# Loading the first key tile of a decode kernel as eight strided loads, with one of them at the head of the load queue

## The chip, the cores and the metric

The kernel runs on one core of a Trainium2 chip. The metric is the device time of one execution in microseconds (us), the median of several runs. Lower is better.

## What is computed

The reference is one decode step of two identical layers. Each layer is an attention block over a key and value cache, followed by a mixing block and an MLP. Batch is 2, there is one query position, the model width D is 576, and there are 32 heads of 128 columns over 16384 cached positions.

```python
def _A_ref(x, k_cache, v_cache, wq, wo):
    q = (x @ wq).reshape(B, Sq, H, Dh).transpose(0, 2, 1, 3)
    scores = jnp.einsum("bhqd,bhkd->bhqk", q, k_cache) * (Dh ** -0.5)
    p = _softmax(scores, axis=-1)
    o = jnp.einsum("bhqk,bhkd->bhqd", p, v_cache)
    return o.transpose(0, 2, 1, 3).reshape(B, Sq, H * Dh) @ wo
...
x = x + _A_ref(_layernorm(x), A_k_cache, A_v_cache, A_wq, A_wo)
x = x + _B_ref(_layernorm(x), B_w1, B_w2, B_w3, B_w4)
x = x + _A_ref(_layernorm(x), A_k_cache, A_v_cache, A_wq, A_wo)
x = x + _B_ref(_layernorm(x), B_w1, B_w2, B_w3, B_w4)
```

Both layers read the same two caches. Each cache is 268 MB, and each layer reads both of them nearly whole, which is almost all of the data that the kernel moves.

## The kernel before

**Tiles.** A unit of work is one pair of heads of one batch entry, so that a layer has 32 units. The keys of a unit are one tile of 128 partitions by 65,536 bytes, 8.4 MB: each of the two heads fills 64 partitions, and each partition takes 256 consecutive positions, which are 64 KB in a row in memory. The values have the same form. The text calls such tiles "a K" and "a V". On-chip memory has room for three of them, in slots that `plan_all` names V, A and C (numbers 0, 1 and 2).

**The order of loads.** All loads are issued by one queue, that of SyncE (SP), in the order in which `plan_all` (L549) lists them in a plan. `Store.pump` (L289) walks through the plan: an entry with a name must find its place free of other owners, and then becomes a load (`Graph.dma`, L85, issued in L98) that writes the memory cells of its place. An entry without a name (`None`) is issued without asking who owns its place, and writes the keys that it lists. The plan starts with the first 128 rows of the query weights wq, then the input x ("xin", two rows), the other four pieces of wq, and the mixer weights w2 in two loads, of which the second goes to the upper 64 partitions only. wq and w2 stand where the first V will be. After them come the tiles: K 0 into slot C, K 1 into slot A, V 0 into slot V as soon as wq and w2 have been used, then K 2 into slot A in two halves as K 1 is used up, and so on, K and V in turn.

**How dependencies become waits.** `Graph._add` (L49) records for each operation the last writer and the readers of each memory cell that it touches. A load that writes a cell which another load wrote depends on that load, though both are issued by the same queue. `Graph._waits` (L118) turns dependencies into semaphore waits, which the queue makes before it issues the load (L182). The semaphore of a load rises by 16 for each of its parts.

**The work.** In `landed` (L1321) GpSimd waits for a tile's load and passes the news on to TensorE and VectorE (the trace shows this as POOLq L187). Then `unit`, in `attention` (L1127), computes the scores of a K tile: a part of it on TensorE (transposes L1414, products L1452), the rest on VectorE (L1499 and L1509, in the first unit L1484 and L1488). The softmax follows, and in the next unit the values are weighted on TensorE (`pv`, L1569, products in L1578). `used` (L1377) and `release` (L329) free the cells that have been consumed, and `release` calls `pump` for the next loads. Before the first unit stand the layer norm of x, the query projection from wq (L930 and L940), a projection from w2 (L993) and the spreading of the first query vector (L1350, L1363, L1367).

The functions that the change touches and what calls them:

Of the kernel before, what the change touches and what calls it, by code (L numbers as in the profile page):

```python
# [338 lines left out]
class KB:  # L339
# [209 lines left out]
    def plan_all(self):  # L549

        B, D = self.B, self.D
        row, w3r, wqr = 2 * D, 2 * self.F, 2 * 128 * self.H
        g = [row * n + CELL for n in self.GROUPS[1]]
        self.cuts, self.korder = {}, {}
        s = [self.slot(i) for i in range(self.NSLOT)]
        source = {"k": self.K, "v": self.V}

        tiles = self.tile_order(0)
        V, A, C = range(3)
        assert tiles[:2] == [("k", 0), ("k", 1)]  # L560
        assert tiles[-3:] == [("k", self.W - 1), ("v", self.W - 2), ("v", self.W - 1)]
        full = lambda k, m, at: (k, 0, m, at)
        hd, mt = self.H, self.MT
        self.store.plan(None, "xin", 0, 0, [(self.rows[0:B, :], self.A_x.rearrange("b s d -> (b s) d"))], ["prod"])
        self.plan_cols("wq", 0, self.wq, [full(k, hd, s[V] + wqr * k) for k in range(self.KT)])
        first = self.store.queue
        first[0], first[1] = first[1], first[0]
        self.plan_small("w2", 0, self.w2, s[V] + wqr * (self.KT - 1) + wqr // 2, (0, 64))
        q = self.TILE // 4
        two = [(2 * q * j, 2 * q) for j in range(2)]  # L570
        assert tiles[3] == ("k", 2)
        for i, (t, u) in enumerate(tiles):
            last = i == len(tiles) - 1
            self.plan_tile(source[t], t, u, C if i == 0 or last else A if t == "k" else V, self.LAST_V if last else two if i == 3 else None)
        r8 = row * self.HG
        assert r8 == w3r

        def halves(n, pieces):
            return [(k, (h or 0) * n // 2, n if h != 0 else n // 2, at) for k, h, at in pieces]
        w = self.WINDOW  # L580
        self.plan_heads(0, w["wo"], 2)
        self.plan_cols("w3", 0, self.w3, halves(mt, w["w3"]))
        self.plan_groups(0, w["w4"])
        self.plan_cols("wq", 1, self.wq, halves(hd, w["wq"]))

        tiles = self.tile_order(1)
        assert tiles[:2] == [("k", self.W - 2), ("k", 0)] and tiles[2] == self.partly()
        tiles[:3] = tiles[2], tiles[0], tiles[1]
        e = self.HOLD * self.CH * 256
        self.plan_tile(source["k"], *tiles[1], A, [(0, e)])  # L590
        self.plan_tile(source["v"], *tiles[0], V, self.REST)
        self.plan_tile(source["k"], *tiles[1], A, [(e, q - e)] + [(q * j, q) for j in range(1, 4)])
        self.plan_tile(source["k"], *tiles[2], C, two)
        assert tiles[4][0] == "v" and tiles[5][0] == "k"
        for i, (t, u) in enumerate(tiles[3:]):
            self.plan_tile(source[t], t, u, C if i == len(tiles) - 4 else A if t == "k" else V, two if i in (1, 2) else None)
        assert t == "v"
        a = s[V]
        ats = []
        for _, lo, hi in self.cuts["wo", 0][-2:]:  # L600
            ats.append(row * (hi - lo))
        ats = [r8] * (self.ng - 1) + ats
        ats = [a + sum(ats[:i]) for i in range(len(ats))]
        self.plan_heads(1, ats)
        a += r8 * self.ng
        self.plan_small("w1", 1, self.w1, a, (0, 64))
        a += row * self.KT
        self.plan_cols("w3", 1, self.w3, [full(k, mt, a + w3r * k) for k in range(self.KT)])
        a += w3r * (self.KT - 1) + w3r // 2
        assert a % CELL == 0 and a + sum(g) <= self.size  # L610
        self.plan_groups(1, [a + sum(g[:i]) for i in range(len(g))], CELL)
# [1055 lines left out]
```

## Time and profile before

| what | value |
|---|---|
| median of 3 runs | 2544.99 us |
| lowest and highest run | 2544.64 and 2546.85 us |
| the profiled execution's own time | 2544.06 us |
| its span, from first to last instruction | 2542.3 us |
| mean granted TensorE clock | 0.639 of full speed |
| read from main memory | 1092.44 MB |

The profile is of one execution. Its views are these. The page has the busy time of each engine (PE is TensorE, PEld its weight loads, DVE VectorE, ACT ScalarE, POOL GpSimd, SP SyncE), the span in 40 equal slices with the busy share in tenths, and the DMA queues. The chain of waits follows the work that ended last back to what released it. The timeline lists instructions with their start and duration, where a q behind an engine's name means its instruction queue. The stages view gives busy time, granted clock, the busy share of the 16 DMA engines and the rate in GB/s for stretches of time. The DMA view counts packets by size in such a stretch and gives the time that they took as a share of 16 engines' time. A packet is counted with its whole time and size where it starts, so that in a short stretch the share can exceed 100%.

### The profile page before, as it was taken

To read this page: it belongs to the slowest core of one execution; us is meant where nothing else is said; L and a number is where in the kernel's file an instruction comes from. 1 tells how busy PE (TensorE), PEld (TensorE's weight loads), DVE (VectorE), ACT (ScalarE), POOL (GpSimd) and SP (SyncE) were. 2 spreads that over 40 slices of the span, in tenths; PEclk is the share of its full clock that TensorE was granted. 3 is DMA by queue.
4 is the path that set the end of the run, shared out by engine and by line. 5 is a ranking of instruction groups with operands and counts; after the bars stand their busy time and mean duration, and the time that the engine had idled before them with its cause. 6 is when DMAs were issued, how large, how long until landed. Compare 5 with 4: busy or idle time off the path is not lost.

```text
span 2542.3 us, 74308 instructions
## 1 busy us (share of the span) xinstructions
PE 1426.8 (56%) x34671; PEld 1335.1 (53%) x34671; DVE 1766.0 (69%) x1122; ACT 1125.9 (44%) x1705; POOL 29.6 (1%) x100
## 2 busy tenths in 40 slices
PE   4655654654655555556678555555465465555555
PEld 3554554544554545545567555455455455455555
DVE  4876866866767767768439777686686686776773
ACT  3553453543544534534447445345354354453451
POOL 0000000000000000000000000000000000000000
PEclk9665665665666666656656666566566666666665
DMA  9999999999999999999999999999999999999999
GB/s 416 431 432 431 439 433 429 440 430 433 430 440 430 431 434 437 432 430 440 403 406 428 436 432 434 435 431 433 435 435 429 435 433 435 431 436 434 431 432 376
DMA packets 28946, 1093.26 MB, mean 430 GB/s; under 512 B 3162, under 2 KB 4828, under 8 KB 9436
## 3 DMA queue, kind: packets, MB, share of 16 engines
q1 hardware_dynamic: 28892, 1092.45, 99.7%
q8 instruction: 45, 0.74, 0.1%
q14 instruction: 9, 0.07, 0.0%
HBM read 1092.44 MB, written 0.00 MB: 430 GB/s over the span
## 4 chain that ended last, share of the span: by engine, by line
DMA 76%; PE 18%; issue 3%; DVE 2%; SPq 1%; ACT 0%; POOLq 0%; DVEq 0%; POOL 0%
DMA mem<-in_A_v_cache_dram 72%; PE mps L1578 17%; DMA mem<-in_A_k_cache_dram 2%; SPq L98 1%; DMA mem<-in_B_w_dram 1%; DVE s_dve L1509 1%; DVE mem L1499 1%; DMA mem<-in_A_wo_dram 1%; DMA mem<-in_A_wq_dram 0%; PE tps L1414 0%; PE sps L930 0%; PE sps L1022 0%; PE sps L1468 0%; PE sps L1560 0%; PE mps L1022 0%
## 5 line engine op out<-in xcount | busy, mean ns | idle before, releaser
L1432 ACT ACTIVATE mem<-tps 128x1024 bf16<-128x1024 bf16 x832 | 810.6, 1099 | 539.7 <-PE tps L1414 536.6
L1509 DVE TENSOR_REDUCE s_dve<-mem 128x32 f32<-128x4096 bf16 x232 | 1024.8, 4417 | 4.0
L1414 PE MATMUL tps<-ident,mem 128*128 128x128 bf16 x6752 | 599.5, 250 | 722.0 <-POOLq L187 722.0
L1499 DVE TENSOR_TENSOR mem<-mem 128x4096 bf16<-128x4096 bf16 x232 | 516.0, 2286 | 595.7 <-POOLq L187 595.7
L1414 PEld LDWEIGHTS tps<-ident,mem 128*128 128x128 bf16 x6752 | 489.5, 114 | 727.5 <-POOLq L187 727.2
L1578 PE MATMUL mps<-p,mem 128*128 128x2 bf16 x16384 | 450.1, 165 | 88.8 <-POOLq L187 67.8
L1578 PEld LDWEIGHTS mps<-p,mem 128*128 128x128 bf16 x16384 | 443.7, 104 | 100.8 <-POOLq L187 71.8
L1452 PE MATMUL sps<-q_col,mem 128*128 128x2 bf16 x8176 | 360.2, 165 | 157.0 <-ACT mem L1432 134.0
L1452 PEld LDWEIGHTS sps<-q_col,mem 128*128 128x128 bf16 x8176 | 301.4, 98 | 221.0 <-ACT mem L1432 213.3
L1543 ACT ACTIVATE mx<-mx 128x2 f32<-128x2 f32 x64 | 13.0, 203 | 597.3 <-POOL mx L1534 597.3
L1432 ACT ACTIVATE mem<-sps 128x1024 bf16<-128x1024 bf16 x174 | 195.8, 1125 | 0.0
L1414 PE MATMUL sps<-ident,mem 128*128 128x128 bf16 x1488 | 135.2, 244 | 0.4 <-DVE prod L1077 0.4
L1414 PEld LDWEIGHTS sps<-ident,mem 128*128 128x128 bf16 x1488 | 107.9, 112 | 0.5 <-DVE prod L1077 0.5
L1367 ACT ACTIVATE mem<-sps 128x128 bf16<-128x128 f32 x63 | 17.4, 277 | 164.2 <-PE sps L1363 164.2
L1488 DVE TENSOR_REDUCE s_dve<-prod 128x16 f32<-128x2048 bf16 (+1 forms) x36 | 80.2, 2227 | 1.2
L1363 PE MATMUL sps<-ident,q_col 128*64 128x128 bf16 x126 | 20.1, 314 | 103.6 <-DVE q_col L1350 103.6
L1484 DVE TENSOR_TENSOR prod<-mem 128x2048 bf16<-128x2048 bf16 (+1 forms) x36 | 43.0, 1195 | 38.8 <-POOLq L187 37.4
L1363 PEld LDWEIGHTS sps<-ident,q_col 128*64 128x64 bf16 x126 | 8.3, 128 | 108.9 <-DVE q_col L1350 108.8
L1547 ACT ACTIVATE p<-s_dve,mx 64x128 bf16<-64x128 f32 (+2 forms) x126 | 54.6, 434 | 13.6 <-PE sps L1560 5.5
L1534 POOL PARTITION_ALL_REDUCE mx<-mx x64 | 25.0, 390 | 2454.0 <-DVE mx L667 2454.0
L1553 ACT ACTIVATE p<-sps,mx 64x128 bf16<-64x128 f32 (+2 forms) x128 | 51.3, 401 | 2.3
L1528 DVE TENSOR_REDUCE mx<-sps 64x1 f32<-64x128 f32 (+2 forms) x128 | 36.6, 286 | 2.6 <-PE sps L1452 1.7
(119 smaller groups left out, 332.6 us busy)
## 6 DMA issues: line engine op xcount, KB each, us to landing
mem<-in_A_k_cache_dram SPq DMA_DIRECT2D x6, 4096.0 KB, 16.7
mem<-in_A_v_cache_dram SPq DMA_DIRECT2D x3, 4096.0 KB, 22.0
mem<-in_A_wq_dram SPq DMA_DIRECT2D x8, 1024.0 KB, 7.8
mem<-in_B_w_dram SPq DMA_DIRECT2D x14, 576.0 KB, 7.3
mem<-in_A_k_cache_dram SPq DMA_DIRECT2D x3, 2048.0 KB, 14.1
mem<-in_B_w_dram SPq DMA_DIRECT2D x7, 864.0 KB, 20.9
mem<-in_B_w_dram SPq DMA_DIRECT2D x4, 1152.0 KB, 17.5
mem<-in_A_v_cache_dram SPq DMA_DIRECT2D x2, 2048.0 KB, 48.5
```

Source lines behind the costliest of these rows:

```text
L1363: ins = pe.matmul(qps[e * h:(e + 1) * h, :], lhsT=q, rhs=self.ident[:, :], start=True, stop=True, skip_group_check=True)
L1414: ins = pe.transpose(out[:, j * 128:(j + 1) * 128], buf[:, j * 128:(j + 1) * 128], self.ident[:, :])
L1432: self.act(lambda e: e.activation(out=self.kt[k], in_=src.rearrange("p (i c) -> p i c", i=self.CH), func=ACT.Copy), reads=bk, writes=self. ...
L1452: ins = pe.matmul(self.sps[sp][:, b:b + 2], lhsT=kt[:, j, :], rhs=self.q_col[:, 2 * sp:2 * sp + 2], start=True, stop=True, skip_group_chec ...
L1484: self.dv(lambda e: e.tensor_tensor(out=prod, in0=buf.rearrange("p (j d) -> p j d", d=128), in1=qbc, op=ALU.mult), reads=self.spilt(("qb", ...
L1488: self.dv(lambda e: e.tensor_reduce(out=sd[:, c0:c0 + DB], in_=prod, axis=AX.X, op=ALU.add), reads=["prod"], writes=self.spilt(("s_dve", m ...
L1499: self.dv(lambda e: e.tensor_tensor(out=prod, in0=buf.rearrange("p (j d) -> p j d", d=128), in1=qbc, op=ALU.mult), reads=self.spilt(("qb", ...
L1509: self.dv(lambda e: e.tensor_reduce(out=sd[:, c0:c0 + n], in_=prod, axis=AX.X, op=ALU.add), reads=pk, writes=self.spilt(("s_dve", m)), to= ...
L1528: self.dv(lambda e, i=i: e.tensor_reduce(out=self.mx[i * h:(i + 1) * h, m, 1:2], in_=self.sps[m][i * h:(i + 1) * h, i:2 * n:2], axis=AX.X, ...
L1547: self.act(lambda e, i=i, at=at: e.activation(out=two(self.p[at, :, i])[:, :, pb:], in_=two(self.s_dve[m][at, 0:self.NB - n]), func=ACT.Ex ...
L1553: self.act(lambda e, i=i, at=at: e.activation(out=two(self.p[at, :, i])[:, :, 0:pb], in_=two(self.sps[m][at, i:2 * n:2]), func=ACT.Exp, bi ...
L1578: ins = pe.matmul(self.mps[:, 448:450], lhsT=buf[:, j * 128:(j + 1) * 128], rhs=self.p[:, b0 + j, :], start=b0 + j == 0, stop=b0 + j == se ...
```

## The change

K 0 is no longer one load of 128 partitions. It becomes eight loads of 16 partitions each: load i writes the partitions i, i + 8, i + 16 up to i + 120, from the same rows of the cache as before, 1 MB each. The first of them is put at the very head of the plan, ahead of wq's first piece and x. The other seven stand in the plan as one nameless entry at the place where K 0 was asked for, ahead of K 1. All eight count on the same semaphore, and all are recorded as writers of the whole slot C.

```diff
+        rows = self.K[0, 0:2].rearrange("h (p j) d -> (h p) (j d)", p=self.HALF)
+        n = 128 // 16
+        place = self.mem[:, s[C] // 2:(s[C] + self.TILE) // 2]
+        by = [(place[i:128:n, :], rows[i:128:n, :]) for i in range(n)]
+        self.store.plan(("k", 0), f"tile{C}", s[C], self.TILE, [(lambda m: by[0][0], by[0][1])])
         self.store.plan(None, "xin", 0, 0, [(self.rows[0:B, :], self.A_x.rearrange("b s d -> (b s) d"))], ["prod"])
         self.plan_cols("wq", 0, self.wq, [full(k, hd, s[V] + wqr * k) for k in range(self.KT)])
         first = self.store.queue
-        first[0], first[1] = first[1], first[0]
+        first[1], first[2] = first[2], first[1]
...
         for i, (t, u) in enumerate(tiles):
             last = i == len(tiles) - 1
+            if i == 0:
+                self.store.plan(None, f"tile{C}", 0, 0, by[1:], self.store.key(s[C], self.TILE))
+                continue
```

## The prediction

> **What bounds the kernel now.** I read the page first: the busy shares, the slices, the queues and the chain.
>
> ```profile
> span 2542.3 us, 74308 instructions
> ...
> PE 1426.8 (56%) x34671; PEld 1335.1 (53%) x34671; DVE 1766.0 (69%) x1122; ACT 1125.9 (44%) x1705; POOL 29.6 (1%) x100
> ...
> DMA  9999999999999999999999999999999999999999
> GB/s 416 431 432 431 439 433 429 440 430 433 430 440 430 431 434 437 432 430 440 403 406 428 436 432 434 435 431 433 435 435 429 435 433 435 431 436 434 431 432 376
> ...
> q1 hardware_dynamic: 28892, 1092.45, 99.7%
> ...
> DMA 76%; PE 18%; issue 3%; DVE 2%; SPq 1%; ACT 0%; POOLq 0%; DVEq 0%; POOL 0%
> ```
>
> No compute engine is busy for more than 69%, but the 16 DMA engines are at 9 tenths or more in every slice and at 99.7% over the span. The kernel is a stream of 1092 MB at 430 GB/s, and an edit counts only if it changes how fast, or how soon, bytes flow. The missing 0.3% of 2542.3 us is 7.6 us. The next view, busy time by stage, shows where it lies.
>
> ```profile
> core 0: us, PE busy (x) PEld busy (x) DVE busy (x) ACT busy (x) POOL busy (x), PEclk, DMA share, GB/s
> 0.00:1.75 1.75, 0.00 (x0) 0.00 (x0) 0.18 (x3) 0.96 (x1) 0.43 (x6) 1.00 0.00 0
> 0.00:5.00 5.00, 0.00 (x0) 0.00 (x0) 0.18 (x3) 1.28 (x1) 0.43 (x6) 1.00 0.59 210
> ...
> 130.00:160.00 30.00, 20.60 (x496) 19.68 (x497) 25.52 (x10) 15.05 (x17) 0.00 (x0) 0.67 0.99 430
> 37.00:52.00 15.00, 13.92 (x248) 12.08 (x248) 14.46 (x9) 13.80 (x16) 0.00 (x0) 1.00 0.99 429
> 2537.00:2542.30 5.30, 2.64 (x73) 2.28 (x73) 0.56 (x3) 0.38 (x2) 0.00 (x0) 0.50 0.14 53
> ```
>
> Nothing moves for the first 1.75 us, and in the last 5.3 us only 0.14 of the engines is in use, which idles 4.6 us. Together that is 6.3 of the 7.6 us. In between (0.99 in both stretches) the engines have no slack in which added transfer time could vanish. The timeline of the queue that issues the loads, and the chain of waits, say how the start is ordered.
>
> ```profile
> 0.79 0.40 SPq L98 DMA_DIRECT2D mem<-in_A_wq_dram  x1
> 1.25 0.32 SPq L98 DMA_DIRECT2D prod<-in_A_x_dram  x1
> 1.63 1.90 SPq L98 DMA_DIRECT2D mem<-in_A_wq_dram  x4
> 3.57 1.08 SPq L98 DMA_DIRECT2D mem<-in_B_w_dram  x2
> 4.69 2.65 SPq L98 DMA_DIRECT2D mem<-in_A_k_cache_dram  x2
> 19.34 0.33 SPq L98 DMA_DIRECT2D mem<-in_A_v_cache_dram  x1
> 69.19 5.30 SPq L98 DMA_DIRECT2D mem<-in_A_k_cache_dram  x2
> ```
>
> ```profile
> 4.69 32.34 DMA mem<-in_A_k_cache_dram
> ...
> 37.56 22.37 issue
> ```
>
> The first K is asked for at 4.69 us and has landed at 37.03 us (4.69 + 32.34). SP is by then some 30 us ahead of the data, and the next V is asked for only when wq and w2 have been used, at 19.34 us.
>
> **The change part by part.** Totals of bytes don't change. One megabyte of the first K moves to the head, the other seven are issued where the whole K was.
>
> *Price of one packet.* For two short stretches the DMA view counts the packets.
>
> ```profile
> DMA packets 16, 1.05 MB, mean 749 GB/s; under 512 B 0, under 2 KB 0, under 8 KB 0
> ...
> q1 hardware_dynamic: 16, 1.05, 173.1%
> ```
>
> ```profile
> DMA packets 155, 1.18 MB, mean 873 GB/s; under 512 B 26, under 2 KB 139, under 8 KB 139
> ...
> q1 hardware_dynamic: 155, 1.18, 231.0%
> ```
>
> The first is 17.9 to 19.3 us, in which each of the 16 engines starts its second packet of the first K: 1.731 x 16 x 1.40 us / 16 = 2.42 us for one row of 64 KB, 27 GB/s an engine, and 16 x 27 is the rate of the page. The whole K is 128 such rows, 8 for an engine, 8 x 2.42 = 19.4 us. The second stretch is 15.3 to 16.65 us: each engine's first K packet, beside the last of w2, whose final load is the only one here that goes to 64 partitions, the upper half (x's two rows and the output aside). All packets together took 2.310 x 16 x 1.35 = 49.9 us. The 113 packets of 1152 bytes need some 51 ns each; that is worked out from the stretch just before, 14 to 15.3 us:
>
> ```profile
> DMA packets 413, 0.50 MB, mean 387 GB/s; under 512 B 10, under 2 KB 400, under 8 KB 413
> ...
> q1 hardware_dynamic: 413, 0.50, 106.0%
> ```
>
> (1.060 x 16 x 1.30 = 22.0 us, less some 2.1 us for 13 packets of 4 KB at 27 GB/s and their overhead, over 390.) So 113 x 0.051 = 5.8 us, and 44.1 us is left for the 16 K packets, 2.75 us each, 0.33 us over the 2.42. The sixteen lengthened by 5.3 us in all, about what the small packets that ran beside them needed. Packet time was paid one for one, as if both shared a way in. It isn't proof: small packets followed by large ones could cost as much by themselves.
>
> *Eight loads of every eighth partition.* Each is 16 rows, one for an engine. The trace shows no such load. From below, a row costs what it costs now, 2.42 us, and the eight loads cost nothing extra. If what an engine may write depends on where its row lies, sixteen rows chosen by one step don't spread as all 128 do, and two engines that end on one way in take 4.84 us for a row each: 8 x 2.42 = 19.4 us more, 2.4 of it in the first load and 17.0 in the seven. Groups of four would make it 3 x 19.4 = 58 us. The nearest row is the stretch beside w2's half-width load, where overlapping packets paid one for one, so I take the pair: +19.4 us.
>
> [...]
>
> *The head.* In the first 5 us 210 x 5 = 1.05 MB starts; at 430 GB/s from 1.75 us on it would be 1.40 MB. The 0.35 MB short are 0.8 us. With 16 long packets in place of 128 short ones all engines should be occupied sooner. Saved: between 0 and 0.8 us; I take 0.4.
>
> *What is pushed back.* wq, x and w2 land later by the first load's time, 2.4 us, or 4.8 if its rows take twice as long. The query vector's chain follows them, and V is asked for at about 22 to 25 us instead of 19.34. What hides it is this wait of PE, which goes on until the first K:
>
> ```profile
> PE tps L1414 <- POOLq L187: 15.0, 1, 15.0
> ```
>
> 15.0 us of waiting against 4.8: nothing. Without that cover every us of it would show. V's own delay is covered by the two Ks ahead of it, 2 x 19.4 us of transfer.
>
> *A wait.* The seven loads write the same cells as the first, so SP waits for that one to land before it issues them. Queued behind it on SP are the second K and all later loads. A megabyte at the head landed thus:
>
> ```profile
> mem<-in_A_wq_dram SPq DMA_DIRECT2D x1, 1024.0 KB, 4.8
> ```
>
> That is 0.79 + 4.8 = 5.6 us, and some 2.4 us more for paired rows, 8 us. SP would have come there at about 5.2 us (4.69 plus one issue), so it waits 0.4 to 3 us. Seven issues instead of one, at the 0.33 us of V's row to the 0.48 of wq's (1.90 / 4), add 2 to 2.9 us. By then 1.0 + 4.7 + 0.7 MB are ahead in the queue, at 430 GB/s until about 16.7 us, longer with paired rows. Cost nothing; if SP were late by over 6 us, each further us would cost one.
>
> *End marks.* Seven more loads end on each engine seven more times. Between 0 and the 51 ns of a small packet each, 0 to 0.36 us; I take 0.1.
>
> *Downstream.* The first K lands 19.4 - 0.4 + 0.1 = 19.1 us later, at about 56 us, and the second K and V, behind it in the same queue, equally. The chain at 37 to 60 us starts with that landing, so the releases that let SP ask for the third K at 69.19 us move by the same 19.1 us, and no gap opens or closes.
>
> Sum against the profiled execution, 2544.06 us (span 2542.3 and 1.76 around it): 2544.06 + 19.1 = 2563.2. The median of the runs shown is 0.93 above the profiled one, 2544.99, which makes 2564.1 us.
>
> **Rivals.** *No collision.* Each engine keeps its 27 GB/s wherever its row lies. For it: 16 long packets are the same descriptors that the whole K consists of, in other grouping, and from 24 to 34 us, with the engines no longer in step, a row still takes 0.984 x 16 x 10 / 65 = 2.42 us:
>
> ```profile
> DMA packets 65, 4.26 MB, mean 426 GB/s; under 512 B 0, under 2 KB 0, under 8 KB 0
> ...
> q1 hardware_dynamic: 65, 4.26, 98.4%
> ```
>
> Then only -0.4 + 0.1 is left: 2543.8 profiled, 2544.7 by the median, not slower. It decides if the first load's 16 rows take 2.4 us side by side.
>
> *Collision in part.* Pairs drift out of step, or the shared way carries more than one engine's 27 GB/s; a row takes 2.9 to 4.4 us: 8 x 0.5 to 8 x 2.0, +4 to +16 us, 2549 to 2561. Against it: sixteen engines that start together on equal rows have no reason to drift.
>
> *Fours.* Four engines to one way: +58 us, 2603. The stretch beside w2, with half the partitions, shows nothing near it.
>
> **How the numbers follow.** Pairs 0.66, in part 0.09, fours 0.03, no collision 0.22. A measurement of this kernel can tell about 0.2% from no change, 5.1 us. The whole start before the full rate is worth 1.75 + 0.8 = 2.6 us, so faster by over 5.1 us has no mechanism: 0.01. Within it lies the rest of no collision, 0.21. Slower are the other three, 0.78. Pairs by themselves give 2560 to 2567 (the head 0 to 0.8, end marks to 0.4, a few us if the collision isn't quite complete, or if runs spread upward as the 2546.85 did). Leaving out no collision would leave out over 2 in 10, so the range goes down to it, 2543.5 to 2567, and leaves out the fours.
>
> **What would show it.** Right: between about 20 and 50 us, in the stretch of the first K, the DMA share stays near 1 while GB/s falls to about 215, and a K packet there takes 4.8 us; the first K lands near 56 us; every later piece of the chain is the same length, 19 us later. The first 16 packets start together soon after 1.8 us, and SP stands at its wait until 7 to 8 us. Wrong: 430 GB/s in that stretch and a landing near 37 us means that where a row lies doesn't matter; a gap in the DMA row before 20 us means that the wait starves the queue; a later V with idle DMA after 60 us means that the covers above were too short.

## The result and the profile after

The changed kernel takes 2566.01 us (median of 6 runs, 2564.83 to 2566.59) against 2544.81 us for the kernel before (6 runs, 2543.22 to 2546.85). The ratio is 1.0084, with a 95% interval of 1.0074 to 1.0094: 21.2 us slower. The profiled execution of the changed kernel took 2566.59 us, with a span of 2564.8 us. The profile's line numbers behind the change are 8 higher than before, because of the added lines. From its page:

```profile
span 2564.8 us, 74315 instructions
...
DMA  9999999999999999999999999999999999999998
GB/s 265 433 434 433 434 432 435 432 434 432 434 432 434 433 434 432 434 432 435 422 397 424 434 437 430 436 430 436 431 435 431 435 432 434 433 433 434 432 434 368
...
q1 hardware_dynamic: 29004, 1092.45, 99.7%
```

The DMA engines are as busy as before, 99.7%, and the bytes are the same. Only the first slice, 64 us long, moved 265 GB/s where it was 416. So busy engines moved fewer bytes there. The DMA view of 28 to 38 us, inside the transfer of the first K, shows how:

```profile
DMA packets 64, 2.10 MB, mean 210 GB/s; under 512 B 32, under 2 KB 32, under 8 KB 32
...
q1 hardware_dynamic: 64, 2.10, 100.3%
```

32 of the packets are under 512 B, the marks at the end of a load (the queue has 112 packets more than before, 29004 against 28892, 16 for each of the seven added loads), so 32 are rows of 64 KB, and each took 1.003 x 16 x 10 / 32 = 5.02 us. Before, a row took 2.42 us. The timeline of SP's queue and the chain of waits place it in time:

```profile
0.79 0.62 SPq L98 DMA_DIRECT2D mem<-in_A_k_cache_dram  x1
1.48 0.56 SPq L98 DMA_DIRECT2D mem<-in_A_wq_dram  x1
2.09 0.32 SPq L98 DMA_DIRECT2D prod<-in_A_x_dram  x1
2.46 2.10 SPq L98 DMA_DIRECT2D mem<-in_A_wq_dram  x4
4.60 3.48 SPq L98 DMA_DIRECT2D mem<-in_B_w_dram  x2
8.79 5.74 SPq L98 DMA_DIRECT2D mem<-in_A_k_cache_dram  x8
25.91 0.33 SPq L98 DMA_DIRECT2D mem<-in_A_v_cache_dram  x1
```

```profile
0.79 7.98 DMA mem<-in_A_k_cache_dram
...
13.31 47.05 DMA mem<-in_A_k_cache_dram
...
60.89 22.37 issue
...
111.56 26.05 DMA mem<-in_A_v_cache_dram
```

The first K has landed at 60.36 us (13.31 + 47.05) instead of 37.03. The piece behind it is again 22.37 us long. The load of the second V starts at 111.56 us. In the kernel before it is this line:

```profile
88.09 26.75 DMA mem<-in_A_v_cache_dram
```

Near the end, the last V of the second layer is waited for in this line of the changed kernel's chain

```profile
2470.13 32.63 DMA mem<-in_A_v_cache_dram
```

and in this one of the kernel before:

```profile
2448.71 32.11 DMA mem<-in_A_v_cache_dram
```

It is asked for 21.4 us later and has landed 21.9 us later (2470.13 + 32.63 against 2448.71 + 32.11). The difference is there in full by 60 us, and all but 1 to 2 us of it is carried to the end.

### The profile page after: what moved, and what is told of

Same layout as the page of the kernel before. It is cut to its first block, busy times and chain, and to the rows that moved or that the text cites. A ratio compares the mean times of both kernels' runs of the same rounds, so it can differ in the third digit from the quotient of the medians.

```text
span 2564.8 us, 74315 instructions
## 1 busy us (share of the span) xinstructions
PE 1427.3 (56%) x34671; PEld 1335.0 (52%) x34671; DVE 1765.9 (69%) x1122; ACT 1126.1 (44%) x1705; POOL 29.6 (1%) x100
## 3 DMA queue, kind: packets, MB, share of 16 engines
q1 hardware_dynamic: 29004, 1092.45, 99.7%
## 4 chain that ended last, share of the span: by engine, by line
DMA 76%; PE 18%; issue 3%; DVE 2%; SPq 2%; ACT 0%; POOLq 0%; DVEq 0%; POOL 0%
DMA mem<-in_A_v_cache_dram 71%; PE mps L1586 17%; DMA mem<-in_A_k_cache_dram 3%; SPq L98 2%; DMA mem<-in_B_w_dram 1%; DVE s_dve L1517 1%; DVE mem L1507 1%; DMA mem<-in_A_wo_dram 1%; DMA mem<-in_A_wq_dram 0%; PE tps L1422 0%; PE sps L938 0%; PE sps L1030 0%; PE sps L1476 0%; PE sps L1568 0%; PE mps L1476 0%
## 6 DMA issues: line engine op xcount, KB each, us to landing
mem<-in_A_v_cache_dram SPq DMA_DIRECT2D x3, 4096.0 KB, 20.8
mem<-in_B_w_dram SPq DMA_DIRECT2D x7, 864.0 KB, 21.4
```

## The experiments

Three theories stood at the start. *Ways in*: what counts is which partitions are written at the same moment, because groups of partitions share a way in. *Source*: rows 512 KB apart in main memory, read at the same time, clash there. *Number*: loads of 16 rows, or many loads, are slow by themselves. The diffs are against the changed kernel, where nothing else is said. Times are compared with the kernel before on the same chip.

**The source in order (e1).**

```diff
-        by = [(place[i:128:n, :], rows[i:128:n, :]) for i in range(n)]
+        by = [(place[i:128:n, :], rows[16 * i:16 * i + 16, :]) for i in range(n)]
```

> As the changed kernel, but each of the eight loads reads 16 successive rows of the cache, 1 MB in a row, instead of every eighth row; the partitions that it writes are the same (the keys of the first K lie in other partitions than the reference has them). Theory of the ways in (what counts is which partitions are written at the same time, two engines to one way): nothing changes, a row takes 5.1 us between 25 and 55 us, the first K lands at 60 us, the total is about 21 us above the kernel before. Theory of the source (rows 512 KB apart in main memory, read at the same time, clash there): a row takes 2.4 us, the first K lands at 37 to 38 us, the total is within 2 us of the kernel before. Theory of the number (loads of 16 rows cost more, whatever they write): 5.1 us and 60 us as with the ways.

2565.69 us against 2544.06 us, ratio 1.0085 (1.0068 to 1.0101). From 29.8 to 31.6 us:

```profile
DMA packets 30, 0.98 MB, mean 546 GB/s; under 512 B 15, under 2 KB 15, under 8 KB 15
...
q1 hardware_dynamic: 30, 0.98, 267.1%
```

15 rows took 2.671 x 16 x 1.8 / 15 = 5.13 us each, though each load read 1 MB in a row. The theory of the source has fallen.

**Sixteen neighbours (e2).**

```diff
+        by = [(place[16 * i:16 * i + 16, :], rows[16 * i:16 * i + 16, :]) for i in range(n)]
```

> As the changed kernel, but each load has 16 neighbouring partitions (0 to 15, 16 to 31, ...), source and place alike. [...] Theory of the source: no rows 512 KB apart, so 2.4 us a row and no loss. Theory of the number: the same 5.1 us a row and the same 21 us as the changed kernel.

2600.27 us against 2544.06 us (one run), 56.2 us slower, and TensorE starts on the first K at 94.80 us. From 60 to 64 us:

```profile
DMA packets 30, 0.98 MB, mean 246 GB/s; under 512 B 15, under 2 KB 15, under 8 KB 15
...
q1 hardware_dynamic: 30, 0.98, 219.2%
```

2.192 x 16 x 4 / 15 = 9.35 us a row. As many loads of as many rows as the change, yet 9.35 us a row against its 5.02. That speaks for the ways in and against the number. By that theory a row of 9.35 us, 3.9 times the 2.42, would be four engines to a way, an estimate from these two row times. The prediction's *Fours* has four times 2.42 us and +58; the run stayed a little below both.

**Every fourth partition (e3).** All loads stand at the K's old place, in one named entry of the plan; the head is taken out.

```diff
-        by = [(place[i:128:n, :], rows[i:128:n, :]) for i in range(n)]
-        self.store.plan(("k", 0), f"tile{C}", s[C], self.TILE, [(lambda m: by[0][0], by[0][1])])
+        by = [(place[i:128:4, :], rows[i:128:4, :]) for i in range(4)]
...
-                self.store.plan(None, f"tile{C}", 0, 0, by[1:], self.store.key(s[C], self.TILE))
+                self.store.plan(("k", 0), f"tile{C}", s[C], self.TILE, [(lambda m, x=x: x[0], x[1]) for x in by])
```

> The first K as four loads of every fourth partition (32 rows, two for an engine), all four at the place where the whole K was asked for, none at the head. [...] If what counts is which ways are written at the same moment, it depends on which rows an engine gets: with two neighbouring rows of the load for each engine, all engines write first to one half of the ways and then to the other, 5.1 us a row, about 20 us slower; with the rows dealt out as those of a whole K are, 2.4 us and no loss. Theory of the number: fewer loads than eight, so less than the 21 us lost.

2543.29 us against 2544.06 us, ratio 0.9997 (0.9987 to 1.0007). From 24 to 34 us:

```profile
DMA packets 98, 4.33 MB, mean 433 GB/s; under 512 B 32, under 2 KB 32, under 8 KB 32
...
q1 hardware_dynamic: 98, 4.33, 100.0%
```

66 rows at 1.000 x 16 x 10 / 66 = 2.42 us. A step of 4 instead of 8 costs nothing that can be measured. If the theory of the ways holds, the rows of such a load are not dealt to the engines in runs of two neighbours: at each moment the engines would then write every eighth partition, as in the changed kernel, where a row took 5.02 us.

**None at the head (e4).** The plan of e3 with the eight loads of the change.

> The eight loads of the change, all at the place where the whole K was asked for, none at the head, and SP does not wait between them. Theory of the ways in: the loss is in the rows, wherever they stand: 5.1 us a row in 8 rounds, 21 us above the kernel before, the first K at about 58 to 60 us. If the head and the wait for it were part of the loss (the first packets start 0.4 us later in the changed kernel, and one engine lags 2.3 us), it is 1 to 3 us less than with the change, 18 to 20 us. Theory of the source and of the number: as with the change, 21 us.

2566.27 us against 2544.06 us, ratio 1.0085 (1.0068 to 1.0102). TensorE starts on the first K at 59.17 us, 1.3 us sooner than in the changed kernel (60.46), but the total is the same within its interval. The loss is in the rows, not in their place at the head.

**Every seventh partition (e5).** Also with the plan of e3.

```diff
+        by = [(place[i:112:7, :], rows[i:112:7, :]) for i in range(7)] + [(place[112:128, :], rows[112:128, :])]
```

> The first K as seven loads of every seventh partition (i, i + 7, ... i + 105; 16 rows, one for an engine) and one load of the 16 partitions 112 to 127, all at the place where the whole K was asked for. [...] If loads of 16 rows with a step between them are slow as such, all rows of the seven loads take 5.1 us and the total is 24 us or more above.

2565.66 us against 2543.56 us (one run): 22.1 us slower. The mean row of each round below took longer than 2.42 us and less than 5.1, so loads of 16 rows with a step are not slow as such, at 5.1 us for every row; in the mildest round most rows took 2.9 us. Three rounds, in the DMA view from 19.3 to 21.1 us (the second load), from 31.8 to 32.65 us (the fifth) and from 34.7 to 36.3 us (the sixth):

```profile
DMA packets 32, 1.05 MB, mean 583 GB/s; under 512 B 16, under 2 KB 16, under 8 KB 16
...
q1 hardware_dynamic: 32, 1.05, 258.2%
```

```profile
DMA packets 26, 0.85 MB, mean 1002 GB/s; under 512 B 13, under 2 KB 13, under 8 KB 13
...
q1 hardware_dynamic: 26, 0.85, 301.0%
```

```profile
DMA packets 28, 0.92 MB, mean 573 GB/s; under 512 B 14, under 2 KB 14, under 8 KB 14
...
q1 hardware_dynamic: 28, 0.92, 244.3%
```

The mean row took 4.65 us (2.582 x 16 x 1.8 / 16), 3.15 us (3.010 x 16 x 0.85 / 13) and 4.47 us (2.443 x 16 x 1.6 / 14). The fourth load is the other mild round. From 28.5 to 30.4 us:

```profile
DMA packets 32, 1.05 MB, mean 552 GB/s; under 512 B 16, under 2 KB 16, under 8 KB 16
...
q1 hardware_dynamic: 32, 1.05, 169.6%
```

That is 1.696 x 16 x 1.9 / 16 = 3.22 us a row. Single rows of the fifth load differ. One started between 32.0 and 32.1 us, eight between 32.1 and 32.5, and one between 32.5 and 32.6:

```profile
q1 hardware_dynamic: 2, 0.07, 259.8%
```

```profile
q1 hardware_dynamic: 16, 0.52, 365.7%
```

```profile
q1 hardware_dynamic: 2, 0.07, 287.2%
```

The eight took 2.93 us on average (3.657 x 16 x 0.4 / 8), the two single ones 4.16 and 4.60 us. Which partitions a packet writes, the trace doesn't say, so which of these rows shared a way isn't shown. If a row on a shared way takes some 5.02 us, as in the changed kernel, the eight had ways of their own, an estimate from these row times, and still took 2.93 us instead of 2.42. The theory of the ways in stands with that addition: these rows speak against its form in which only the sharing engines pay.

**Every fourth with the first load at the head (e6).** The changed kernel's plan, with four loads.

```diff
+        by = [(place[i:128:4, :], rows[i:128:4, :]) for i in range(4)]
```

> The change with every fourth partition instead of every eighth: four loads of 32 rows, 2 MB each, the first at the head of all loads, SP waiting for it before it issues the other three. Every fourth partition cost nothing at the K's place, so this times the head and the wait alone. If the first packets start sooner with few long rows: 0.4 to 0.8 us faster, which is within 0.2%. By the profile of the changed kernel, in which the first packets started at 2.2 us instead of 1.8: 0 to 0.5 us slower, within 0.2% too. If the wait or the later wq cost anything, the first K lands more than 1 us later than the 37.0 us of the kernel before.

2543.78 us against 2543.56 us, ratio 1.0002 (0.9993 to 1.0011), and TensorE starts on the first K at 37.32 us. The head brings nothing that can be measured. The wait isn't tested here: SP had finished with w2 only at 9.09 us (4.60 + 4.49 in its timeline) and issued the next part of K at 9.13, so that it found the first load landed. For the wait there is e4, which has neither head nor wait, and the same total as the change.

**The second K too (e7).**

```diff
+            if i == 1:
+                more = self.K[1, 0:2].rearrange("h (p j) d -> (h p) (j d)", p=self.HALF)
+                spot = self.mem[:, s[A] // 2:(s[A] + self.TILE) // 2]
+                self.store.plan((t, u), f"tile{A}", s[A], self.TILE, [(lambda m, i=i: spot[i:128:n, :], more[i:128:n, :]) for i in range(n)])
+                continue
```

> The change, and the second K as eight loads of every eighth partition as well, all at its place. Theory of the ways in: the loss comes a second time, 8 rows of 5.1 instead of 2.42 us, 21.4 us, and nothing hides it: 42 to 45 us above the kernel before; the second K lands about 41 us after the first instead of 19.4. If part of a late landing is taken up by slack behind the first K, or if the loss were that of the start, less: 21 to 35 us.

2589.81 us against 2543.56 us (one run), 46.2 us slower. TensorE's rows in the timeline, at the first and the second K:

```profile
59.98 2.74 PE L1427 MATMUL tps<-ident,mem 128*128 128x128 bf16 x24 [31.22 <-POOLq L187]
...
100.66 3.60 PE L1427 MATMUL tps<-ident,mem 128*128 128x128 bf16 x32 [15.28 <-POOLq L187]
```

40.7 us lie between the two, instead of a transfer of 19.4 us. The loss came twice and nothing hid it. The total is 1.2 us above the expected 42 to 45; what makes the rest isn't shown.

**w2's narrow load first (e8).** The diff is against the kernel before.

```diff
-        self.store.plan((nm, l), nm, at, 2 * KT * D, [
+        two = [
...
+        self.store.plan((nm, l), nm, at, 2 * KT * D, two[::-1] if nm == "w2" else two)
```

> The kernel before, with the two loads of w2 in the other order: the narrow one (64 rows, upper half of the partitions) first, the 512 rows of full width after it, so that the first packets of the first K run beside full-width loads alone. The prediction read the 2.75 us of those 16 packets, 0.33 over the usual 2.42, as the price of sharing ways in with the narrow load. If so, they now take 2.42 to 2.5 us. If it is the change from short packets to long ones, they still take 2.6 to 2.8 us. The total is within 1 us of the kernel before in both cases.

2543.13 us against 2543.56 us (one run). The first packets of the first K, from 15.55 to 16.75 us:

```profile
DMA packets 148, 1.18 MB, mean 985 GB/s; under 512 B 16, under 2 KB 132, under 8 KB 132
...
q1 hardware_dynamic: 148, 1.18, 234.6%
```

All packets took 2.346 x 16 x 1.2 = 45.0 us. The 116 short ones at 51 ns need 5.9 us, which leaves 2.45 us for each of the 16 rows, where the same reading of the kernel before gave 2.75. Beside full-width loads nothing lengthens. It was the narrow load.

**Two halves (e9).** The plan of e3.

```diff
+        by = [(place[64 * i:64 * i + 64, :], rows[64 * i:64 * i + 64, :]) for i in range(2)]
```

> The first K as two loads of 64 neighbouring partitions (0 to 63, then 64 to 127), both at the place where the whole K was asked for. [...] If the rows of a load are dealt to the engines so that only four ways are in use at a time: 9.3 us a row, about 56 us above. If only loads of 16 rows are slow: 2.4 us a row and no loss.

2567.97 us against 2543.56 us (one run), 24.4 us slower. From 36 to 46 us:

```profile
DMA packets 43, 2.03 MB, mean 203 GB/s; under 512 B 12, under 2 KB 12, under 8 KB 12
...
q1 hardware_dynamic: 43, 2.03, 98.3%
```

31 rows at 0.983 x 16 x 10 / 31 = 5.07 us. Loads of 64 rows are as slow as those of 16 with a step of 8 (5.02 us), as two engines to a way would be, and not the 9.3 us of four. TensorE starts on the first K at 60.80 us, against 59.17 in e4.

**Columns (e10).**

```diff
+        by = [(place[:, 4096 * i:4096 * i + 4096], rows[:, 4096 * i:4096 * i + 4096]) for i in range(n)]
```

> The change with the cut turned: eight loads of all 128 partitions and 8 KB of each, 1 MB a load, the first at the head, the others at the K's place, with the same wait of SP. Theory of the ways in (extended by what the runs so far showed: any shared way slows all engines): no way is shared, so packets of 8 KB take 0.31 us, the first K lands at 37 to 38 us, the total is within 0.2% of the kernel before. If eight loads, their end marks, the head or the wait cost something by themselves: 1 us or more above, up to the 21 us of the change.

2543.79 us against 2543.56 us, ratio 1.0 (0.999 to 1.0009). Eight loads, one of them at the head and with the same end marks, cost nothing that can be measured when each goes to all 128 partitions. (The others depend on the first as in the change, but SP came to them at 5.88 us, when it had landed.) With this the theory of the number has fallen for many loads. For loads of 16 rows it falls by e2 and e5, where such loads took 9.35 and 3.15 us a row, and by e9, where loads of 64 rows are just as slow, 5.07 us a row. No load of 16 rows with rows of 2.42 us is shown by these readings.

## Why the prediction was right, and where its sizes were off

*The direction and the price* held: a row took 5.02 us instead of 2.42, about half the rate, as two engines on one way into the memory would have it. No trace shows a way or which engine ends on which, so the pair stays the author's reading of the row times. The choice of partitions written is shown as the cause by e1 (another source, same loss), e10 (as many loads over all partitions, no loss) and e3 (another step, no loss). The argument from the row beside w2's narrow load is confirmed by e8. *No collision* and *collision in part* are refuted. The row time of *Fours* is nearly met in e2, 9.35 us. The stated range says less: from 2543.5 to 2567 us it held no change at all too, and 2566.01 lies 1 us below its top. The prediction also let only the engines on a shared way pay. e5 speaks against that, with eight rows at 2.93 us beside two at 4.16 and 4.60. For the forecast it made little difference: the mean row of the change took 5.02 us, near the pair's 4.84.

*The pair's price* was the term that was mis-sized: 4.84 us a row, 19.4 us in all. A row took 5.02 us, more than twice the 2.42 of a row of the whole K: 8 x (5.02 - 2.42) = 20.8 us. That accounts for 1.4 of the 2.1 us between the forecast of 19.1 and the measured 21.2. Another 0.9 us stood in no term: the first 15 rows of the second K took 3.39 us on average, while one late engine still wrote the first K (shown in the last section), 15 x (3.39 - 2.42) / 16 = 0.9 us. The two make 21.7 us. The medians are 21.2 us apart, the two profiled executions 22.5.

*The head* was taken as a gain of 0.4 us. The stages view of the changed kernel has the same rate in the first 5 us as before, 210 GB/s, with the engines at 0.99 instead of 0.59:

```profile
0.00:5.00 5.00, 0.00 (x0) 0.00 (x0) 0.18 (x3) 1.28 (x1) 0.43 (x6) 1.00 0.99 210
1.75:7.00 5.25, 0.00 (x0) 0.00 (x0) 0.00 (x0) 0.32 (x1) 0.00 (x0) 1.00 0.96 204
```

The view counts a packet whole where it starts, and the 16 rows of the first load last beyond the 5 us (they have landed at 8.77), so the equal rate hides a loss: from 1.75 to 7 us it is 204 GB/s, in the kernel before 347. The long rows kept the engines busy, but took 4.94 us each (16 rows at 151.9% in the DMA view from 1.75 to 5 us, 1.519 x 16 x 3.25 / 16). SP's issue of the first load took 0.62 us, where wq's 128 rows took 0.40. That goes with the step, and not with few long rows: e6's step of 4 took 0.56, e2's 16 neighbours and e10's columns 0.40. Without the collision, e6 and e10 show no gain either. A gain of 0.4 us would be lost in the noise of their times, but TensorE started on the first K at 37.32 and 37.53 us, no sooner than the 37.13 of the kernel before. So this term is best put at 0.

*End marks* were taken as 0.1 us. By e10 they cost nothing that shows, in a time that is known to some 2.5 us.

*The wait* came as described, but for other reasons of time. SP had finished with w2 only at 8.08 us (4.60 + 3.48, where w2's two issues took 1.08 before), and the first load landed at 8.77, so that it waited 0.7 us, within the 0.4 to 3 forecast. Why w2's issues took longer isn't shown. The queue did not run dry: from 1.75 to 7 and from 7 to 12 us the engines are at 0.96.

*What is pushed back* stayed hidden: V was asked for at 25.91 us, just past the 22 to 25 forecast, and TensorE still waited 31.75 us for the first K:

```profile
60.46 2.74 PE L1422 MATMUL tps<-ident,mem 128*128 128x128 bf16 x24 [31.75 <-POOLq L187]
```

*The landing* was expected 19.1 us later and came 23.3 us later. Part of that isn't lost time of the stream, but one late engine: between 53 and 55 us the DMA view shows a single row starting.

```profile
DMA packets 2, 0.07 MB, mean 33 GB/s; under 512 B 1, under 2 KB 1, under 8 KB 1
```

That row took some 5.3 us (the stretch is at 16.7%, 0.167 x 16 x 2), and the load landed at 60.36 us, while the other engines were on the second K from 55.4 us on. So the next V landed 22.8 us later (111.56 + 26.05 against 88.09 + 26.75 in the chain of the kernel before), the last V of the second layer 21.9 us later, and the two profiled executions end 22.5 us apart (2566.59 and 2544.06). What moves this distance by a microsecond or so behind the landing wasn't tried.

*Downstream* was right: the loss passed to the end nearly whole, and e7 doubled it.

## What to carry to other kernels

In this kernel, whose DMA engines are busy for 99.7% of the span, how the first K's loads lie over the partitions set what they cost: with the same bytes and the same number of loads, a step of 8 cost 21 us, 16 neighbours 56 us, and columns over all 128 partitions nothing that could be measured. When a tile has to be cut into loads, cut it along the row and leave each load all 128 partitions, as e10 did (2543.79 us against 2543.56), or choose a cut that the chip was timed with (every fourth partition did no harm in e3, 2543.29 us against 2544.06). The page shows such a loss only as GB/s falling, here from 416 to 265 in the first slice, while the DMA share stays at 9, so read the two rows together.

## What the runs showed of the hardware

In these runs, rows beside slower ones took longer than 2.42 us, though less than 5. In e5's fifth load eight rows took 2.93 us on average beside two of 4.16 and 4.60. The means there were 3.22 and 3.15 us a row in the fourth and fifth loads and 4.65 and 4.47 in the second and sixth, and in the change, with a step of 8, it is 5.02 us. The changed kernel shows it once more where the late engine still writes its last row while the others are on the second K, from 55.4 to 56.8 us:

```profile
DMA packets 30, 0.98 MB, mean 702 GB/s; under 512 B 15, under 2 KB 15, under 8 KB 15
...
q1 hardware_dynamic: 30, 0.98, 226.9%
```

15 rows took 2.269 x 16 x 1.4 / 15 = 3.39 us on average, and two rounds later, from 61.5 to 63 us, 16 rows took 2.42 us again:

```profile
DMA packets 16, 1.05 MB, mean 699 GB/s; under 512 B 0, under 2 KB 0, under 8 KB 0
...
q1 hardware_dynamic: 16, 1.05, 161.4%
```

If the change has two engines on a way, these move 2 x 65.5 KB in 5.02 us, 26.1 GB/s, less than the 27 of an engine in the whole K (65.5 KB in 2.42 us); if e2 has four, they move 4 x 65.5 KB in 9.35 us, 28.0 GB/s. Both are estimates from those row times. Which partitions share a way, why rows of 2.93 us in e5 and 3.39 us in the change were held up, and by which rule the rows of a load of 32 or 64 partitions are dealt to the engines, these runs leave open.
